# Top-32 attention with two feed-forward layers on one core: the scores of the tile two steps on move from the end of TensorE's step to between its first and second unit

## The chip, the core and the metric

The kernel runs on one core of a Trainium2 chip. The core has five engines that work side by side: TensorE (matmuls), VectorE, ScalarE, GpSimd and SyncE, which here issues nearly all DMAs. Each engine takes its own instructions in the order in which the program lists them, and waits at an instruction until what it needs is there. The metric is the device time of one execution in microseconds (us).

## What is computed

```python
scores = q @ k.T / sqrt(64)                    # 4 batches x 8 heads, 576 x 576
kth    = the 32nd largest of each row of scores
attn   = softmax(where(scores >= kth, scores, -1e9))
x      = attn @ v                              # 2304 tokens x 512
h      = max(x @ w1, x @ w2, x @ w3)           # dense layer, 768 wide
x      = h @ w_out
e      = argmax(x @ w_gate)                    # one of 8 experts per token
out    = gate_weight * (relu(x @ ew1[e]) @ ew2[e])
```

Everything is float32. The kernel keeps precision by splitting a float32 operand into two float16 halves, so that one product takes three matmuls.

## The kernel before, in words

**Tiles and steps.** The score matrix is cut into 144 tiles of 128 rows by 576 columns: 128 "full" ones, and 16 "pair" ones that hold two rests of 64 rows. One loop over `t` (line 1601 and on) is a software pipeline: step `t` does each stage of the attention for another tile. Stages that matter here: the scores of tile `t + 2` (`st_scores`, TensorE, L892), the evacuation of the scores of tile `t + 1` from PSUM to SBUF (`st_evac`, ScalarE, L899), the search for the largest values (`st_chunks` and others, VectorE, L921), threshold passes (ScalarE L967 and L1042, GpSimd L973 and L1045), the exponential and its split in halves (L1051, L1062, L1066), the transpose by DMA (`st_ptr`, SyncE's queue, L1071), and the product with v of tile `t - 14` (`st_av`, TensorE, L1085). Tiles form groups of four; the AV products of a group share one PSUM tile (one buffer), which VectorE reads once the group is done (L1134). The score tile `S` in PSUM has one buffer too, so the scores of tile `t + 2` must wait for the evacuation of tile `t + 1`.

**Units.** When the attention of 128 tokens is done, their dense layer becomes a job of ten units for TensorE: six of `unit_h` (a third of half the dense layer each, 36 matmuls on L355 through the helper `turned`), two of `unit_x2` (the second dense matrix, 9 matmuls on L1178 to L1180), `unit_gate` (12 short matmuls, L1200 to L1202) and `unit_rank` (2 short ones, L1244 and L1245, for the place of each token in its expert's list). Later there are also units of an expert's layers: `unit_e1` (24 matmuls on L355) and `unit_e2` (6 on L366 to L368). A unit writes one of four PSUM tiles `mm`. What reads it is put on the list of the next step or of a later one (`after(1, post)`): a ScalarE copy (L1160 for every third `unit_h`, L1185, L1435), a VectorE maximum (L1163) or a chain of small VectorE operations. In ScalarE's order of a step these copies stand ahead of that step's evacuation, `st_evac`.

**How many units a step does.** `run_units` adds a rate to a credit (1.08 a step at first, later 1.4 and 1.8) and runs units while the credit is positive; a unit of the dense layer costs 1.0, one of an expert 0.67, a gate 0.25 and a rank 0.05. So most steps do one or two big units, and the gate or the rank comes as a small unit ahead of a big one.

**TensorE's order in a step.** Normally: AV, units, four warm-up matmuls on L1710 if credit is left over, scores. In a step where a new group of AV products begins (`fresh`, every fourth), the units come first, then AV, warm-up and scores. These lines of the loop make that order:

```python
if fresh:
    open_slots()
    load_ahead()
    run_units(t)
if ok(n):
    st_av(n)
...
if ok(t + 2):
    st_scores(t + 2)
```

`open_slots` and `load_ahead` issue DMAs on SyncE's queue; `run_units` and `st_scores` issue none. When the attention is over (about 655 us) the loop goes on with units alone, and after it `finale` works off the lists of the experts (from about 787 us).

Of the kernel before, what the change touches and what calls it, by code (L numbers as in the profile page):

```python
# [19 lines left out]
def kernel(  # L20
# [23 lines left out]
    KE = FE // P  # L44
# [13 lines left out]
    UNIT_RATE, TAIL_RATE = 1.08, 2.0  # L58
    NEARLY, NPICK, NMIX, NS1 = 10, 2, 7, 8
    CAP, XA, NSL, NLD, NAHEAD = 1.2, 3, 10, 4, 4  # L60
    NSWAP, XLAG, KLAG, TSTOP, EARLY_RATE, LATE_RATE = 4, 2, 2, 140, 1.4, 1.8
# [33 lines left out]
    def attempt(ctx, general):  # L95
# [18 lines left out]
        def part(n, p=P):  # L114
            o = parts[0]
            parts[0] += n
            return vec[0:p, o:o + n]
# [7 lines left out]
        first = part(NE, 1)  # L125
# [86 lines left out]
        def look_ahead(snap, m8):  # L212

            return [
                lambda: nc.vector.scalar_tensor_tensor(out=m8, in0=snap, scalar=0.0, in1=vrev[0:1, :],
                                                       op0=ALU.is_gt, op1=ALU.mult),
                lambda: nc.vector.scalar_tensor_tensor(out=m8, in0=first, scalar=0.0, in1=m8, op0=ALU.is_equal,
                                                       op1=ALU.mult),
                lambda: nc.vector.max(out=m8, in_=m8),
                lambda: nc.vector.tensor_scalar(out=ahead, in0=m8[:, 0:1], scalar1=-1.0, scalar2=float(NE),  # L220
                                                op0=ALU.mult, op1=ALU.add),
                lambda: nc.vector.tensor_scalar(out=ahead, in0=ahead, scalar1=float(NE - 1), scalar2=None, op0=ALU.min),
                lambda: nc.vector.tensor_copy(out=aheadi, in_=ahead),
            ]
# [402 lines left out]
        with ExitStack() as p1:  # L627
# [40 lines left out]
            def freed():  # L668
                live[0] -= 1
# [9 lines left out]
            def chain(fns):  # L679
                chains.append(list(fns))  # L680
                return chains[-1]
# [66 lines left out]
            def run_late():  # L748
                while late:
                    late.pop(0)()  # L750
# [132 lines left out]
            def st_scores(n):  # L883
                kind, b, qb, h = tiles[n]
                ps = ps_s.tile([P, 2, 512], F32, tag="S", name="S")
                Sps[n] = ps
                qt, (km, kr) = qT[b, qb], kT[b]
                hs = [(h, 0, P)] if kind == "full" else [(h[0], 0, REM), (h[1], REM, REM)]
                for j in range(2):
                    for vv in range(2):  # L890
                        for hh, o, m in hs:
                            nc.tensor.matmul(out=ps[o:o + m, j, 0:(REM if j else NQ * P)], lhsT=qt[:, vv, hh, 0:m],  # L892
                                             rhs=kr[:, hh] if j else km[:, hh // HG, :, hh % HG],
                                             start=(vv == 0), stop=(vv == 1))
# [392 lines left out]
            slots, task, W1h, W1e, eld, hld = [], [], [], [], [], []  # L1287
            ew, e1, e2, half = [], [], [], [None]
# [55 lines left out]
            def load_ahead():  # L1344

                if not looked:
                    if raw and len(ranked) >= NTT - NAHEAD:
                        looked.append(clock[0])
                        chain(look_ahead(ranked[-1].snap, sm_p.tile([1, NE], F32, tag="m8s", name="m8s")))
                elif looked[0] + 1 < clock[0] and n_raw[0] < 2 * KD and len(eld) == KE + 2 * KD:  # L1350
                    w, i = divmod(n_raw[0], KD)
                    n_raw[0] += 1
                    re = nc.sync.value_load(aheadi[0:1, 0:1], min_val=0, max_val=NE - 1)
                    n = (1, KE // KD)[w]
                    nc.sync.dma_start(
                        out=raw[w][:, i * n:(i + 1) * n, :],
                        in_=(ew1, ew2)[w][bass.ds(re, 1), i * n * P:(i + 1) * n * P, :].rearrange(
                            "o (k p) f -> p (o k) f", p=P))
# [132 lines left out]
            credit = [0.0]  # L1491

            def run_unit():
                if run_early():
                    return True
                for j in jobs:
                    if j.ready > clock[0] or (live[0] >= room() and j.u != NU1 + 1):
                        continue
                    if j.u < NU1:
                        unit_h(j, j.u)  # L1500
                        j.ready = clock[0] + (3 if j.u == NU1 - 1 else 0)
                        credit[0] -= 1.0
                    elif j.u < NU1 + 2:
                        unit_x2(j, j.u - NU1)
                        j.ready = clock[0] + (0 if j.u == NU1 else 4)
                        credit[0] -= 1.0
                    elif j.u == NU1 + 2:
                        unit_gate(j)
                        j.ready = 1 << 30
                        credit[0] -= 0.25  # L1510
                    else:
                        unit_rank(j)
                        credit[0] -= 0.05
                    j.u += 1
                    if j.u == NU1 + 4:
                        jobs.remove(j)
                    return True
                return run_late_slot()

            def run_units(t):  # L1520
                credit[0] = min(credit[0] + (TAIL_RATE if e2 else LATE_RATE if len(eld) >= KE else EARLY_RATE if slots
                                             else UNIT_RATE), 2.5 if e2 else CAP)
                while credit[0] > 0 and run_unit():
                    pass


            preps = []
# [20 lines left out]
            def ok(n):  # L1548
                return 0 <= n < NTL
# [8 lines left out]
            with tc.manual_schedule():  # L1558
# [35 lines left out]
                t = -1  # L1594
# [6 lines left out]
                while second is None or not fin() or len(ranked) < NTT:  # L1601
# [89 lines left out]
                    n = t - L_AV  # L1691

                    fresh = ok(n) and n % G == 0
                    if fresh:
                        open_slots()
                        load_ahead()
                        run_units(t)
                    if ok(n):
                        st_av(n)
                        if n % G == G - 1:  # L1700
                            after(1, lambda g=n // G: st_x(g))
                    if not fresh:
                        open_slots()
                        load_ahead()
                        run_units(t)

                    if WARM and 30 <= t < NTL and credit[0] > 0 and live[0] < room() - 1:
                        ps = mm_tile()
                        for _ in range(WARM):
                            nc.tensor.matmul(out=ps, lhsT=ones16, rhs=WO[:, 0, 0, :], start=True, stop=True)  # L1710
                        freed()
                    if ok(t + 2):
                        st_scores(t + 2)
                    run_late()
                    if not picked and len(ranked) >= NPICK:
                        picked = t
# [22 lines left out]
    with ExitStack() as first_time:  # L1739
        attempt(first_time, False)  # L1740
    with tc.If(missed[0] > 0, preferred_fallthrough_block=False):
        with ExitStack() as second_time:
            attempt(second_time, True)
# [29 lines left out]
```

## Time and profile before

| | us |
|---|---|
| median of 3 runs (923.32 to 924.06) | 924.04 |
| the profiled execution | 919.08 |
| its span, first to last instruction | 917.4 |

| engine | busy us | share of the span |
|---|---|---|
| VectorE (DVE) | 745.3 | 81% |
| TensorE matmuls (PE) | 741.1 | 81% |
| ScalarE (ACT) | 705.7 | 77% |
| GpSimd (POOL) | 597.5 | 65% |

The shares are means over stages with different limits. The first 145 us load and split the weights and start the pipeline, and TensorE does little; from 145 to 652 us attention and units run together; the rest is units and experts. In the views, PE is TensorE, DVE VectorE, ACT ScalarE, POOL GpSimd and SPq the DMA queue of SyncE. A line of a timeline gives start, duration, engine, source line, operation, what is written and read, and the count; in square brackets stands how long the engine had been idle before and what ended that.

### The profile page before, as it was taken

The numbers are of one execution on the slowest core, as the hardware profiler recorded it, in microseconds if no ns is written. First come the engines' busy times: TensorE is split into PE (matmuls) and PEld (weight loads), VectorE is DVE, ScalarE is ACT, GpSimd is POOL, SyncE is SP. The second block draws the span as 40 slices with busy tenths as digits, with TensorE's granted clock in tenths as the row PEclk, the third lists the DMA queues.
The fourth block names the chain that finished last, engine by engine and source line by source line (L and its number), as shares of the span: only waits on it lengthen the run. The fifth ranks groups of instructions, "written<-read, shape, count | busy, mean of one in ns | idle before, by whom it ended". The sixth has DMA issues, their size and how long they took to land.

```text
span 917.4 us, 29131 instructions
## 1 busy us (share of the span) xinstructions
PE 741.1 (81%) x10606; PEld 573.4 (63%) x10606; DVE 745.3 (81%) x3108; ACT 705.7 (77%) x1464; POOL 597.5 (65%) x554
## 2 busy tenths in 40 slices
PE   1112367888878799978988899989999999999993
PEld 0000236576655678757767688757987756687882
DVE  5999998999999999999998999998852426476661
ACT  4768999999999999999997999998862231566661
POOL 2556788898988699887877889888992220211110
PEclk9999999999998999999989999999999999999997
DMA  9872977767997888799989788988977459699270
GB/s 223 262 232 51 222 148 152 128 135 133 194 167 162 157 153 169 150 201 173 175 167 172 167 158 155 179 173 148 188 153 128 128 170 298 173 298 258 60 223 16
DMA packets 372164, 155.93 MB, mean 170 GB/s; under 512 B 331931, under 2 KB 348319, under 8 KB 372000
## 3 DMA queue, kind: packets, MB, share of 16 engines
q1 hardware_dynamic: 368128, 143.10, 75.0%
q0 software_dynamic: 3136, 9.46, 3.3%
q8 instruction: 87, 1.43, 0.7%
q10 hardware_dynamic: 736, 1.32, 0.4%
q14 instruction: 77, 0.63, 0.2%
HBM read 76.06 MB, written 16.67 MB: 101 GB/s over the span
## 4 chain that ended last, share of the span: by engine, by line
PE 29%; ACT 20%; issue 19%; DVE 17%; POOL 8%; DMA 4%; SPq 1%; POOLq 0%; ACTq 0%; DVEq 0%
PE mm L355 15%; ACT g L967 4%; DVE c L921 4%; PE av L1085 4%; ACT s L899 3%; PE S L892 3%; ACT e L1051 3%; ACT phl L1062 2%; POOL phl L1066 2%; DVE vec L982 2%; POOL f L973 2%; PE mm L1178 2%; DVE e L1056 2%; PE mm L1179 2%; PE mm L1180 2%
## 5 line engine op out<-in xcount | busy, mean ns | idle before, releaser
L355 PEld LDWEIGHTS <-W 128*128 128x128 f16 x4560 | 248.5, 100 | 19.6 <-issue 16.5
L355 PE MATMUL mm<-xT,W 128*128 128x128 f16 x3456 | 214.3, 224 | 13.3 <-DVE vl L746 5.6
L973 POOL TENSOR_TENSOR f<-s,g 128x576 f32<-128x576 f32 x144 | 184.1, 1278 | 40.4 <-ACT g L967 24.2
L1066 POOL TENSOR_TENSOR phl<-e,phl 128x576 f16<-128x576 f32 x144 | 188.2, 1307 | 6.5 <-ACT phl L1062 5.7
L921 DVE MAX8 c<-s 128x8 f32<-128x96 f32 x864 | 175.0, 243 | 9.4 <-ACT s L899 5.6
L892 PEld LDWEIGHTS <-qT 128*128 128x128 f16 (+1 forms) x640 | 56.6, 107 | 189.8 <-issue 155.2
L892 PE MATMUL S<-kt,qT 128*128 128x64 f16 (+3 forms) x320 | 61.9, 345 | 107.2 <-ACT s L899 91.5
L1051 ACT ACTIVATE e<-s,be 128x576 f32<-128x576 f32 x144 | 109.8, 762 | 14.6 <-POOL phl L1066 10.9
L1085 PE MATMUL av<-vh,pt 128*128 128x65 f16 (+3 forms) x1600 | 110.6, 200 | 11.4 <-DVE xn L1134 9.8
L967 ACT ACTIVATE g<-s,bf 128x576 uint16<-128x576 f32 x144 | 111.7, 775 | 5.6
L982 DVE MAX8 vec<-f 128x8 f32<-128x576 f32 x144 | 108.7, 755 | 4.7 <-POOL f L973 1.9
L1045 POOL TENSOR_TENSOR s<-s,g 128x576 f32<-128x576 f32 x72 | 92.6, 1286 | 24.0 <-DVE e L1056 22.3
L1085 PEld LDWEIGHTS <-pt 128*128 128x128 f16 (+3 forms) x2400 | 89.3, 103 | 24.2 <-issue 11.0
L899 ACT ACTIVATE s<-S 128x576 f32<-128x576 f32 x144 | 91.6, 636 | 12.3 <-PE S L892 11.9
L1062 ACT ACTIVATE phl<-e 128x576 f16<-128x576 f32 x144 | 96.2, 668 | 5.9 <-DMA pt<-phl 5.9
L1085 PE MATMUL av<-vl,pt 128*128 128x64 f16 (+3 forms) x800 | 100.1, 197 | 0.0
L461 DVE SCALAR_TENSOR_TENSOR W<-st,W 128x1024 f16<-128x1024 f32 x56 | 65.8, 1220 | 37.3 <-ACT W L460 28.7
L1056 DVE SCALAR_TENSOR_TENSOR e<-s,hkth,e 128x576 f32<-128x576 f32 x72 | 85.4, 1186 | 12.7 <-ACT e L1051 8.0
L892 PE MATMUL S<-kT,qT 128*128 128x512 f16 (+3 forms) x320 | 48.6, 292 | 22.5 <-ACT s L899 22.4
L1169 POOL TENSOR_TENSOR hhl<-a,hhl 128x384 f16<-128x384 f32 x36 | 37.6, 1046 | 33.5 <-ACT hhl L1168 32.3
L460 ACT ACTIVATE W<-st 128x1024 f16<-128x1024 f32 x56 | 55.6, 1046 | 1.8 <-DMA st<-in_moe_w_dram 1.8
L1042 ACT ACTIVATE g<-s,hkth 128x576 uint16<-128x576 f32 x72 | 54.7, 760 | 0.0
(233 smaller groups left out, 1568.6 us busy)
## 6 DMA issues: line engine op xcount, KB each, us to landing
st<-in_moe_w_dram SPq DMA_DIRECT2D x72, 512.0 KB
st<-in_moe_w_dram SPq DMA_DIRECT2D x28, 256.0 KB
raw<-in_moe_w_dram SPq DMA_DIRECT2D x12, 512.0 KB
st<-in_v_dram SPq DMA_DIRECT2D x16, 256.0 KB
hs<-he SPq DMA_DIRECT2D x16, 256.0 KB
hTe<-hs SPq DMA_DIRECT2D x8, 512.0 KB
st<-in_q_dram SPq DMA_DIRECT2D x15, 256.0 KB
qT<-qT SPq DMA_DIRECT2D x30, 128.0 KB
```

The lines of the kernel that those rows point to most:

```text
L355: nc.tensor.matmul(out=ps[:, o * n:(o + 1) * n], lhsT=w(b, kk, c), rhs=x(a, kk), start=(kk == 0 and i == 0), stop=(kk == KD - 1 and i == 2))
L892: nc.tensor.matmul(out=ps[o:o + m, j, 0:(REM if j else NQ * P)], lhsT=qt[:, vv, hh, 0:m], rhs=kr[:, hh] if j else km[:, hh // HG, :, hh % HG],
L899: nc.scalar.activation(out=s, in_=Sps.pop(n).rearrange("p a b -> p (a b)")[:, 0:S], func=ACTF.Copy, scale=DOWN)
L921: nc.vector.max(out=c[:, i * 8:(i + 1) * 8], in_=s[:, i * CW:(i + 1) * CW])
L967: nc.scalar.activation(out=gg[n], in_=Ss[n], func=ACTF.Sign, bias=bf[g][:, i], accum_out=cnt[g][:, i])
L973: let_in(nc.gpsimd.tensor_tensor(out=ff[n], in0=Ss[n], in1=gg.pop(n).bitcast(F16), op=ALU.subtract))
L982: bulk.append(lambda: nc.vector.max(out=y8[g][:, i, 1:9], in_=y))
L1051: nc.scalar.activation(out=e, in_=Ss.pop(n) if early(n) else Ss[n], func=ACTF.Exp, scale=ESC, bias=be[g][:, i])
L1056: masked.append(nc.vector.scalar_tensor_tensor(out=e, in0=Ss.pop(n), scalar=kth[g][:, i:i + 1], in1=e, op0=ALU.is_ge, op1=ALU.mult))
L1062: nc.scalar.activation(out=ph[:, 0, 0:S], in_=p, func=ACTF.Copy)
L1066: nc.gpsimd.tensor_tensor(out=ph[:, 1, 0:S], in0=p, in1=ph[:, 0, 0:S], op=ALU.subtract)
L1085: nc.tensor.matmul(out=av[o:o + m, i, 0:n], lhsT=t[0:kk, p * NCH + c, o:o + m], rhs=v_rows(x, b, c, hh)[:, 0:n], start=(c == 0 and p == 0 ...
```

## The change

Scores are emitted between the first unit that a step runs and the others. `run_units` gets an argument: its first call in a step adds the rate to the credit and runs at most one unit, then come the scores, and the second call runs the rest. In a fresh step this whole block stands ahead of the AV product, so the scores come ahead of it too. The warm-up matmuls come behind the scores.

```diff
-            def run_units(t):
-                credit[0] = min(credit[0] + (TAIL_RATE if e2 else LATE_RATE if len(eld) >= KE else EARLY_RATE if slots
+            def run_units(t, first):
+                if first:
+                    credit[0] = min(credit[0] + (TAIL_RATE if e2 else LATE_RATE if len(eld) >= KE else EARLY_RATE if slots
                                              else UNIT_RATE), 2.5 if e2 else CAP)
                 while credit[0] > 0 and run_unit():
-                    pass
+                    if first:
+                        break
...
                     fresh = ok(n) and n % G == 0
-                    if fresh:
+                    def units():
                         open_slots()
                         load_ahead()
-                        run_units(t)
+                        run_units(t, True)
+                        if ok(t + 2):
+                            st_scores(t + 2)
+                        run_units(t, False)
+                    if fresh:
+                        units()
                     if ok(n):
                         st_av(n)
                         if n % G == G - 1:
                             after(1, lambda g=n // G: st_x(g))
                     if not fresh:
-                        open_slots()
-                        load_ahead()
-                        run_units(t)
+                        units()
...
-                    if ok(t + 2):
-                        st_scores(t + 2)
                     run_late()
```

## Rows read from the trace of the kernel before

**Rows 1.** Three stretches: busy us of PE, PEld, DVE, ACT, POOL; clock; DMA.
```profile
145.00:608.00 463.00, 407.56 (x6264) 329.58 (x6263) 438.87 (x2101) 433.51 (x958) 397.13 (x345) 0.97 0.86 163
608.00:655.00 47.00, 46.53 (x623) 34.82 (x623) 42.43 (x210) 41.45 (x92) 41.76 (x35) 0.96 0.95 164
655.00:787.00 132.00, 130.37 (x1585) 94.19 (x1585) 60.09 (x227) 52.54 (x101) 51.78 (x59) 1.00 0.72 173
```
**Rows 2.** Waits, 145 to 608 us (SPq to 655): us, times, longest.
```profile
PE S L892 <- ACT s L899: 31.2, 26, 3.1
ACT s L899 <- PE S L892: 6.7, 9, 1.8
ACT xr L1185 <- PE mm L1180: 2.0, 1, 2.0
DVE c L921 <- ACT s L899: 2.5, 6, 0.9
SPq L1071 <- PE av L1085: 29.7, 19, 4.3
```
**Rows 3.** Timeline of step 118 (fresh), and of one single-unit step.
```profile
545.80 0.63 ACT L899 ACTIVATE s<-S 128x576 f32<-128x576 f32 x1
544.77 4.18 PE L355 MATMUL mm<-xT,W 128*128 128x128 f16 x72
549.60 0.66 PE L892 MATMUL S<-kT,qT 128*128 128x512 f16 x4
550.30 0.65 ACT L899 ACTIVATE s<-S 128x576 f32<-128x576 f32 x1 [1.33 <-PE S L892]
569.55 0.65 ACT L899 ACTIVATE s<-S 128x576 f32<-128x576 f32 x1 [0.44 <-PE S L892]
```
**Rows 4.** Timeline of step 133: second unit, scores, ScalarE's next two.
```profile
615.19 2.17 PE L355 MATMUL mm<-xR,W 128*128 128x128 f16 x36
617.20 0.65 PE L892 MATMUL S<-kT,qT 128*128 128x512 f16 x4
617.69 1.23 PE L355 MATMUL mm<-xR,W 128*128 128x128 f16 x19
617.40 0.49 ACT L1160 ACTIVATE a<-mm 128x384 f32<-128x384 f32 x1 [0.53 <-PE mm L355]
617.89 0.65 ACT L899 ACTIVATE s<-S 128x576 f32<-128x576 f32 x1
```
**Rows 5.** Timeline of step 65: rank, two big units, evacuations, VectorE.
```profile
307.43 0.17 PE L1245 MATMUL mm<-oh,ones 128*128 128x8 f16 x1
311.15 5.81 PE L355 MATMUL mm<-xT,W 128*128 128x128 f16 x72 [3.56 <-DVE vl L746]
312.14 0.63 ACT L899 ACTIVATE s<-S 128x576 f32<-128x576 f32 x1
317.49 0.65 ACT L899 ACTIVATE s<-S 128x576 f32<-128x576 f32 x1 [1.82 <-PE S L892]
317.24 1.20 DVE L1163 TENSOR_TENSOR a<-a,mm 128x384 f32<-128x384 f32 x2
```
**Rows 6.** Timeline of step 137: gate's end, scores, SP, ScalarE.
```profile
630.14 0.17 PE L1202 MATMUL mm<-wg,x2T 128*128 128x8 f16 x1
632.75 0.65 PE L892 MATMUL S<-kT,qT 128*128 128x512 f16 x4
625.19 1.42 SPq L1071 DMA_TRANSPOSE pt<-phl  x1
629.15 0.68 ACT L1062 ACTIVATE phl<-e 128x576 f16<-128x576 f32 x1 [1.26 <-DMA pt<-phl]
631.30 0.64 ACT L899 ACTIVATE s<-S 128x576 f32<-128x576 f32 x1
```
**Rows 7.** Granted clock (figure before the last two), and 72 matmuls.
```profile
311.50:314.00 2.50, 2.50 (x28) 2.50 (x26) 1.48 (x10) 2.50 (x10) 1.07 (x2) 0.51 0.83 188
395.60:399.00 3.40, 3.40 (x62) 3.40 (x62) 3.40 (x18) 3.37 (x9) 2.70 (x3) 1.00 1.07 172
395.57 4.18 PE L355 MATMUL mm<-xT,W 128*128 128x128 f16 x72 [1.66 <-DVE he L1436]
```

## The prediction

> **What bounds the kernel now.** I read the table of stretches first [rows 1]. From 145 to 608 us no engine sets the pace alone: of 463 us VectorE is busy 438.87, ScalarE 433.51 and TensorE 407.56. From 608 to 655 TensorE is busy 46.53 of 47 us, and from 655 to 787, where only units and the last AVs are left, 130.37 of 132. So the kernel has two regimes around this change. Up to 608 us the two softmax engines pace it and TensorE has about 55 us of idle time; from 608 us on TensorE has none, and whatever idle time it is given there goes straight to the end. Before 145 us there are no units and TensorE mostly waits; only the AV of every fourth step changes places with the scores there, and I cost that at nothing.
>
> The table of waits comes next [rows 2]. Up to 608 us TensorE waits 31.2 us in front of the scores for ScalarE's evacuation, since the score tile has one buffer. In the other direction ScalarE waits only 6.7 us, in 9 places, for the scores to be done. The change is about these 9 places. VectorE, which takes the evacuated scores, waits 2.5 us for ScalarE there.
>
> Last I read the timeline of single steps. A step lasts about 4.4 us (106 steps, 26 to 131, in 463 us). Its order on TensorE is AV, units, warm-up matmuls, scores; in every fourth step, where a new group of AV tiles begins ("fresh"), it is units, AV, warm-up, scores.
>
> **What the change does to the order.** No instruction is added or removed. Which unit runs in which step is decided by a credit, and the split call adds it once and takes the same units, so only TensorE's order changes; no DMA is issued in the moved code, and what is issued for later steps (the readers of a unit) hangs on the step, not on the place. From the loops, of steps 14 to 141, 44 plain steps have two or more units and 11 have warm-up matmuls behind at most one: there the scores pass the second unit or the warm-up. All 32 fresh steps change: the scores pass the AV too. The other 41 stay as they are.
>
> **The gain, up to 608 us.** Step 118 is the pattern [rows 3]. ScalarE has emptied the score buffer at 545.80 + 0.63 = 546.43. TensorE does both units (4.18 us from 544.77), the AV, and the scores from 549.60; ScalarE has waited 1.33 us when it can start at 550.30. In the new order the scores start behind the first unit, about 546.9, and ScalarE's wait is gone. The ceiling is the 6.7 us, less 0.44 for a step with a single unit (the row at 569.55) [rows 3], 6.3 us. The floor is what VectorE waits for the same evacuations, 2.5 us [rows 2]: where VectorE has work in hand, an earlier ScalarE gives nothing. I take the middle, 4.4 us.
>
> **The loss, up to 608 us.** ScalarE takes its work in order, and the reader of a step's second unit stands in front of the evacuation of the scores in the next step. That unit now ends later, by the scores it lets pass: 617.69 - 617.20 = 0.49 us from their start to the next matmul [rows 4]. Rows 4 is the pattern: the second unit ends at 617.36 and ScalarE, which had waited 0.53 us for it, copies it at 617.40 and evacuates at 617.89. In the new order that copy starts 0.5 us later and the evacuation behind it too, though its scores are long there: the wait has moved from the scores to the unit. Between 145 and 608 us I find nine steps (33, 59, 71, 95, 96, 100, 101, 104, 105) with such a reader close behind its second unit; with 0.2 us of slack on the mean they cost 9 x 0.3 = 2.7 us. Step 59 among them is ScalarE's wait of 2.0 us [rows 2].
>
> Step 65 is a loss of another kind [rows 5]. Its first unit is the ranking, two short matmuls, over at 307.6. The new order then waits for the evacuation (312.14 + 0.63), where TensorE used to start the two big units at 311.15. They would start at 312.77 + 0.5 = 313.3 and end about 5.81 us later, at 319.1. VectorE reads them at 317.24, two readings of 0.6 us, the second at 317.9: it would wait 1.2 us. ScalarE's 1.82 us there is gained, and counted above. The loss is 2.7 + 1.2 = 3.9 us, and between 0 (if the engines are out of step by more than 0.5 us) and 3.9.
>
> AVs of fresh steps come 0.5 us later as well, and SP's transposes wait for AVs (29.7 us in 19 places [rows 2]), with loads queued behind. I cost it at nothing: what is transposed is read two steps, about 9 us, later. If that cover were gone it would be 19 x 0.5 = 9.5 us on SP, which is not the end of any chain I read. The AV's own wait for VectorE (fresh steps) no longer holds up the scores; that is within the gain counted.
>
> So the first stretch gives -4.4 + 3.9 = -0.5 us.
>
> **The cost, 608 to 655 us.** What ScalarE waits for scores there is worth nothing, since TensorE is the bound. What counts is whether TensorE gets new idle time. In most steps the first unit ends after the evacuation. Step 137 is the exception [rows 6]: its first unit is the gate, which ends at 630.14 + 0.17 = 630.31, and the evacuation runs from 631.30 to 631.94. TensorE used to do two expert units in this time, and scores at 632.75 without a wait. Now it waits at the scores, with the two units behind them in its queue: 631.94 - 630.31 = 1.6 us, 1.7 with the start after a wait (0.04 us between 617.36 and 617.40 [rows 4], an estimate for TensorE). That ScalarE may come earlier to it does not help much: it is held up just before, 1.26 us, by a transpose that SP issued at 625.19. Bounds: 0 (evacuation earlier by the whole 1.7) and 1.7; I take 1.7, since the row of the transpose is in the way.
>
> **The sum.** -0.5 + 1.7 = +1.2 us. The rows are of one execution of 919.08 us (span 917.4 and 1.7 around it), 5.0 us below the median of 924.04; I carry the difference over to the median: 925.2 us, which is within the 0.2% (1.85 us) that a measurement of this kernel can tell from no change.
>
> [...]
>
> **The rivals.**
> - ScalarE paces the first stretch: all of 6.3 us comes back and the late readers cost nothing, because the whole step moves ahead of them. For it: ScalarE's waits are real idle time. Against it: VectorE is the busier engine. 924.0 - 6.3 + 1.7 = 919.4 us, faster. Chance 0.24.
> - The second units become the wait: VectorE's 2.5 us is all that is gained, and the 3.9 and 1.7 us are paid: 924.0 - 2.5 + 3.9 + 1.7 = 927.1 us, slower; with no gain at all 929.6. It decides from the point at which more steps have a reader within 0.5 us of its unit than have a wait for the scores. For it: nine against nine. Chance 0.28.
> - The clock falls in the gap of step 137: TensorE, the bound there, loses 5.81 - 4.18 = 1.6 us more, 926.8 us, slower. Against it: the 1.66 us row. Chance 0.08.
> - The change does next to nothing: TensorE waits 31.2 us at the scores in any order, and the place of a wait is all that moves: 924.0 us. Chance 0.10.
>
> **How the numbers follow.** The forecast of 925.2 has 0.30; with the rival that nothing happens, "within 0.2%" has 0.40. Faster has 0.24, slower 0.28 + 0.08 = 0.36. The range goes from the first rival, 919.4, to the far end of the second, 929.6; beyond these the gains or losses would have to exceed every wait that I found.
>
> **What would show it.** In the profile after: ScalarE's waits for the scores nearly gone (right: under 1.5 us in all up to 655); in their place waits of ScalarE for the matmuls of units, 2 to 5 us; TensorE's waits at the scores longer than 31.2 us, with a new one of over a microsecond in step 137, before two expert units; TensorE still without idle time from there to 787. It would be wrong if VectorE's busy share between 145 and 608 rose above 96% (a real gain), if TensorE showed no new gap behind the gate of step 137, or if SP's transposes came so late that ScalarE waited for them more often than now.

## The result and the profile after

The changed kernel takes 935.39 us (median of 6 runs, 931.38 to 939.88) where the kernel before takes 924.05 us beside it: 1.0115 times as long, 95% interval 1.0084 to 1.0147. The change makes the kernel 11 us slower, and the time lies above the whole predicted range. The profiled execution of after took 932.32 us, with a span of 930.6 us; before it was 919.08 and 917.4, so the two traces differ by 13.2 us.

The stretches of the profile of after, in the columns of [rows 1] (stretch, its length, busy us of PE, PEld, DVE, ACT and POOL, granted clock, share of the DMA engines, GB/s). The last row, of a stretch that is looked at below, is followed by the row of before for the same stretch.

```profile
145.00:608.00 463.00, 400.20 (x6104) 323.14 (x6103) 429.11 (x2061) 424.89 (x938) 388.86 (x337) 0.96 0.83 159
608.00:655.00 47.00, 44.37 (x601) 34.20 (x600) 39.23 (x204) 40.35 (x92) 39.58 (x36) 0.96 0.76 155
655.00:787.00 132.00, 130.30 (x1719) 99.17 (x1717) 62.90 (x251) 54.94 (x112) 59.17 (x64) 1.00 0.74 170
...
392.00:470.00 78.00, 64.13 (x907) 52.77 (x905) 67.10 (x307) 65.87 (x145) 58.60 (x52) 0.91 0.87 171
```
```profile
392.00:470.00 78.00, 65.45 (x955) 54.07 (x954) 74.28 (x347) 74.61 (x166) 64.22 (x58) 0.93 0.98 182
```

Against [rows 1], VectorE and ScalarE have done 9.8 and 8.6 us less work between 145 and 608 us. Most of that is missing in one place, 392 to 470 us, where they do 7.2 and 8.7 us less. Before, both of them and the DMA engines were busy 95 to 98% of that stretch. From 608 to 655 us TensorE has 2.2 us more idle time than before, from 655 to 787 no more.

The waits of after, 145 to 608 us (the last row, SyncE's queue, to 655), answer to [rows 2]: us in total, times, longest.

```profile
PE S L892 <- ACT s L899: 60.1, 45, 4.3
DVE c L921 <- ACT s L899: 6.9, 10, 1.8
ACT a L1160 <- PE mm L355: 5.9, 6, 1.7
ACT xr L1185 <- PE mm L1180: 5.8, 4, 2.3
ACT hl L762 <- DMA kT<-hl: 3.2, 1, 3.2
ACT s L899 <- PE S L892: 3.0, 4, 1.2
ACT he L1435 <- PE mm L355: 2.8, 2, 1.6
...
SPq L1071 <- PE av L1085: 53.5, 24, 6.1
```

ScalarE's waits for scores fell from 6.7 to 3.0 us, which is what the change does. In their place ScalarE waits 14.5 us for units (lines 1160, 1185 and 1435; before 2.2, of which 0.2 on line 1160), TensorE 60.1 us in front of the scores (31.2), SyncE's transposes 53.5 us for AVs (29.7).

Where the time goes can be followed with one measure: the start of ScalarE's evacuation (line 899) of the scores of tile n, after less before. Step t evacuates tile t + 1. From n = 24 to 80 this lag goes up and down and comes back to under 1 us: 0.1 us at 34, 1.9 at 44, 0.1 at 50, -0.7 at 68, 0.8 at 80. Then it is 1.2 us at tile 87, 7.2 at 90, 8.4 at 96, 10.3 at 98 and still 10.3 at 101. It falls to 6.8 at 120, and is 8.6 at 138, 10.3 at 140, 11.6 at 142 and 10.0 at 143, the last. So 9 us come from the steps 86 to 96, and up to 3 from the steps 137 to 141. Near 755 us TensorE is 11.1 us behind; the rest is lost later, where it waits 1.9 us longer in all for two DMAs of the experts' inputs. How far the lag moves by itself can be read from the run with step 137 alone (below): up to that step its order is that of before, and its lag lies between -0.8 us (tile 61) and 2.9 us (tile 127). A smaller change of the lag in a single trace shows nothing by itself.

Step 86 is fresh and begins with a job's ranking. This is TensorE there, and then SyncE's queue (start, duration, engine, line, operation; in brackets the idle time before and what ended it):

```profile
396.83 0.17 PE L1245 MATMUL mm<-oh,ones 128*128 128x8 f16 x1
399.63 1.01 PE L892 MATMUL S<-kt,qT 128*128 128x512 f16 x4 [2.63 <-ACT s L899]
400.45 5.48 PE L355 MATMUL mm<-xT,W 128*128 128x128 f16 x72
```
```profile
405.77 0.19 PE L1085 MATMUL av<-vh,pt 128*128 128x65 f16 x1
```
```profile
398.86 1.62 SPq L1071 DMA_TRANSPOSE pt<-phl  x1
400.53 0.57 SPq L729 DMA_DIRECT2D st<-in_k_dram  x1
401.33 2.08 SPq L784 DMA_TRANSPOSE kT<-hl  x1
406.56 1.32 SPq L1071 DMA_TRANSPOSE pt<-phl  x1
409.39 0.38 SPq L1333 DMA_DIRECT2D st<-in_moe_w_dram  x1
409.87 1.39 SPq L721 DMA_DIRECT2D st<-in_k_dram  x1
411.36 1.48 SPq L784 DMA_TRANSPOSE kT<-hl  x1
```

The kernel before had the same AV, P transpose, loads and K transpose here:

```profile
399.59 0.19 PE L1085 MATMUL av<-vh,pt 128*128 128x65 f16 x1
```
```profile
401.44 1.33 SPq L1071 DMA_TRANSPOSE pt<-phl  x1
404.28 0.38 SPq L1333 DMA_DIRECT2D st<-in_moe_w_dram  x1
404.76 0.94 SPq L721 DMA_DIRECT2D st<-in_k_dram  x1
405.80 1.30 SPq L784 DMA_TRANSPOSE kT<-hl  x1
```

The ranking is over at 397.0. The scores wait 2.63 us for the evacuation, and the two large units stand behind them. Behind these stands the AV: 405.77 us, where before it began at 399.59. SyncE's transpose of the next P tile (line 1071) needs the buffer that this AV reads. It is issued at 406.56 (before 401.44), and the expert-weight load, the K load and the K transpose behind it follow 5 us late as well (before 404.28, 404.76, 405.80). Two engines meet the K transpose:

```profile
416.52 0.63 ACT L762 ACTIVATE hl<-st 64x512 f16<-64x512 f32 x1 [3.18 <-DMA kT<-hl]
```
```profile
417.67 0.68 DVE L746 TENSOR_TENSOR hl<-mm,hl 64x512 f16<-64x512 f32 x1 [2.83 <-ACT mm L745]
```

ScalarE's line 762 splits the next piece of K into a buffer that the late transpose still reads; before, it waited 0.27 us there.

### The profile page after: what moved, and what is told of

It is laid out like the page before. It is cut to its first block, busy times and chain, and to the rows that moved or that the text cites. A ratio compares the mean times of both kernels' runs of the same rounds, so it can differ in the third digit from the quotient of the medians.

```text
span 930.6 us, 29090 instructions
## 1 busy us (share of the span) xinstructions
PE 741.7 (80%) x10606; PEld 575.7 (62%) x10606; DVE 743.0 (80%) x3108; ACT 705.0 (76%) x1464; POOL 596.5 (64%) x554
## 4 chain that ended last, share of the span: by engine, by line
PE 28%; DVE 22%; issue 19%; ACT 18%; POOL 6%; DMA 5%; SPq 1%; POOLq 0%; DVEq 0%; ACTq 0%
PE mm L355 14%; DVE c L921 5%; ACT s L899 3%; PE av L1085 3%; DVE vec L982 3%; PE S L892 3%; DVE e L1056 3%; ACT g L967 3%; ACT e L1051 2%; ACT phl L1062 2%; PE mm L1178 2%; ACT mm L745 2%; PE mm L1180 2%; PE mm L1179 2%; POOL f L973 1%
## 5 line engine op out<-in xcount | busy, mean ns | idle before, releaser
L1085 PE MATMUL av<-vh,pt 128*128 128x65 f16 (+3 forms) x1600 | 108.5, 200 | 0.5 <-DMA pt<-phl 0.3
L1056 DVE SCALAR_TENSOR_TENSOR e<-s,hkth,e 128x576 f32<-128x576 f32 x72 | 82.9, 1151 | 12.3 <-ACT e L1051 11.5
```

The source lines that it names most:

```text
L1056: masked.append(nc.vector.scalar_tensor_tensor(out=e, in0=Ss.pop(n), scalar=kth[g][:, i:i + 1], in1=e, op0=ALU.is_ge, op1=ALU.mult))
L1085: nc.tensor.matmul(out=av[o:o + m, i, 0:n], lhsT=t[0:kk, p * NCH + c, o:o + m], rhs=v_rows(x, b, c, hh)[:, 0:n], start=(c == 0 and p == 0 ...
```

## Experiments

Two theories for the 11 us. **A, the late AV:** in a fresh step the AV comes behind the scores' wait and the held-up units; SyncE's queue stands still until it is done, and the loads behind come late. **B, the late units:** large units stand behind the scores' wait, and their readers on ScalarE and VectorE come late, over many steps. Most kernels below choose for each step the old or the new order, by this edit of the changed kernel and one condition:

```diff
+                    split = CONDITION
                     def units():
...
-                        if ok(t + 2):
+                        if split and ok(t + 2):
                             st_scores(t + 2)
...
                         freed()
+                    if not split and ok(t + 2):
+                        st_scores(t + 2)
                     run_late()
```

Each time is a median, with the kernel before timed beside it on the same chip (it took 918.5 to 921.6 us in these groups); the ratio has its 95% interval. It is taken from all the runs of the two kernels, so it need not be the quotient of the two medians. The expectations give times for a kernel before of 924 us; where it took 921.3 beside the first four runs, they are read here as differences from it.

**The old order in fresh steps.**

```diff
+                    split = not fresh
```

> The changed kernel, but the 32 fresh steps keep the old order (all units, AV, scores). Theory A (late AV): in a fresh step the AV now stands behind the scores and the held-up units, SP's next P transpose waits for that AV, and the loads and K transposes queued behind it come late to ScalarE; this is some 9 of the 11.3 us. Expected by A: 925 to 928 us, what is left being the gap of step 137. Theory B (late second units): the loss comes from units held up behind the scores' wait, in plain and fresh steps alike, whose readers on ScalarE and VectorE come late: 931 us or more.

928.84 us, ratio 1.0086 (1.0065 to 1.0107), 7.5 us above before, where A had 1 to 4 and B 7 or more: B's figure, and a miss for A as the only cause. In its trace the lag still grows from 3.4 us (tile 87) to 7.5 (tile 98), three quarters of it from tile 92 on, in plain steps.

**The old order in step 86.**

```diff
+                    split = t != 86
```

> The changed kernel, with the old order in step 86 alone. Step 86 is fresh and begins with the ranking, so that the scores' wait, two units and the AV stood behind each other there. Theory A (late AV), if this one step begins the loss: 926 to 929 us, and the trace shows no wait of ScalarE's split for the K transpose near 417 us. Theory B (late second units, spread over many steps): 934 to 935.5 us.

926.83 us, ratio 1.0062 (1.0040 to 1.0083), 5.5 us above before; A had 2 to 5 and B 10 or more. ScalarE's wait for the K transpose there falls from 3.2 to 1.0 us, and between tiles 87 and 101 the lag grows by 3.6 us instead of 9.0. So roughly half of that is step 86, and the rest is something else.

**The new order in step 86 alone.**

```diff
+                    split = t == 86
```

> The kernel before, with the new order in step 86 alone. Theory A (late AV): most of the loss is made here, 929 to 933 us. Theory B (late second units over many steps): 924 to 926 us.

925.36 us, ratio 1.0050 (1.0028 to 1.0072). One step costs some 4 us, between B's 0 to 2 and A's 5 to 9. Its trace shows the chain again, TensorE first and then ScalarE (the first of ScalarE's three waits, at 402.87, is for a K transpose issued at 400.74, ahead of the held one, and is not part of the chain):

```profile
399.04 1.12 PE L892 MATMUL S<-kt,qT 128*128 128x512 f16 x4 [4.48 <-ACT s L899]
399.96 5.64 PE L355 MATMUL mm<-xT,W 128*128 128x128 f16 x72
```
```profile
402.87 0.63 ACT L762 ACTIVATE hl<-st 128x512 f16<-128x512 f32 x1 [1.66 <-DMA kT<-hl]
409.47 0.65 ACT L899 ACTIVATE s<-S 128x576 f32<-128x576 f32 x1 [1.45 <-PE S L892]
415.34 0.63 ACT L762 ACTIVATE hl<-st 64x512 f16<-64x512 f32 x1 [2.32 <-DMA kT<-hl]
```

**Gate and ranking don't count as first unit.** The scores come behind the first large unit, which covers the evacuation.

```diff
...
-                    if first:
+                    if first and big[0]:
                         break
```

(`big` is set when the unit took more than half a credit.)

> The changed kernel, but gate and ranking don't count as a step's first unit: the scores come behind the first large unit. In steps 86, 92 and 137 a large unit then covers the evacuation. Theory A (late AV): the AV of step 86 is late by the scores alone, 0.5 us, so the loss there goes, and so does the gap of step 137: 923 to 926 us. If already an AV that is 0.5 us late blocks SP, as fresh steps have it everywhere: 930 us or more. Theory B (late second units): only the 18 steps with a gate or a ranking first are changed, a gain of 3 to 5 us: 930 to 932 us.

921.74 us, ratio 1.0005 (0.9986 to 1.0025), which is A's figure (-1 to 2 us above before) and not B's (6 to 8): the loss is not spread over all steps, but lies in steps whose first unit is a gate or a ranking. Within those steps it tells nothing between a late AV and late units, since both are on time again.

**Step 86, the AV ahead of the scores.** Only the AV moves against the run with step 86 alone: ranking, AV, scores, two units.

```diff
+                    split = t == 86
...
+                        if split:
+                            st_av(n)
                         if split and ok(t + 2):
                             st_scores(t + 2)
...
                     if ok(n):
-                        st_av(n)
+                        if not split:
+                            st_av(n)
```

> The kernel before, with step 86 alone in the order ranking, AV, scores, the two large units. Against the run with step 86 alone in the new order (4.0 us slower than before) only the AV moves, ahead of the scores' wait; the two units stay held up behind it. Theory A (the late AV blocks SP): SP's transpose of step 87 is issued at 401 to 402 us instead of 406.2, the late K transpose goes, and of the 4 us no more than 2 are left. Theory B (the late units): SP is early as in A, but the time stays 3.5 to 5 us above before.

920.21 us, ratio 1.0008 (0.9992 to 1.0023). The units stay late, and ScalarE waits for one of them and for late scores (waits of ScalarE, 396 to 425 us: total, times, longest):

```profile
ACT a L1160 <- PE mm L355: 2.5, 1, 2.5
ACT s L899 <- PE S L892: 0.9, 1, 0.9
```

The lag rises from 0.5 us at tile 87 to 4.1 at tile 89 and is back to 2.0 at tile 92: of what the late units lose here, the next steps make good about half in the trace, and by time 0.7 us are left, which can't be told from nothing. The transpose of line 1071 is issued at 401.93, and no wait for the K transpose is left. Step 86 is A's.

**Steps 92 and 96 alone.**

```diff
+                    split = t in (92, 96)
```

> The kernel before, with the new order in steps 92 and 96 alone: plain steps, the first with the gate, the second with the ranking as first unit. In the changed kernel with the old order in step 86 the evacuations fell 3.6 us back between steps 87 and 103. If that is these two steps: 3 to 4 us above before, with ScalarE waiting for the large unit of step 92 and for the expert unit of step 95 or 96. If it is the sum of many small delays in plain steps with two large units: 0 to 1 us above before.

922.69 us, ratio 1.0031 (1.0011 to 1.0050), in accord with the first expectation. Step 92, with the gate first, in its trace (the first fence TensorE and its granted clock over the held-up unit, the second ScalarE):

```profile
429.59 1.12 PE L892 MATMUL S<-kt,qT 128*128 128x512 f16 x4 [1.41 <-ACT s L899]
...
430.60:433.40 2.80, 2.80 (x37) 2.80 (x35) 2.70 (x16) 2.25 (x4) 2.79 (x3) 0.65 0.55 125
```
```profile
433.71 0.49 ACT L1160 ACTIVATE a<-mm 128x384 f32<-128x384 f32 x1 [0.86 <-PE mm L355]
438.89 0.65 ACT L899 ACTIVATE s<-S 128x576 f32<-128x576 f32 x1 [1.25 <-PE S L892]
```

The unit runs at a granted clock of 0.65 and takes 3.15 us instead of 2.17 (before, at 1.00), its reader waits 0.86 us, and two steps on the scores themselves are late, 1.25 us. The lag grows by 2.3 us at tiles 94 and 95 and keeps that to tile 101; step 96 adds 0.2. ScalarE's two waits are for a late unit and for scores that stand behind units, as B has it. SyncE's transpose waits for a late AV here too (3.6 us in one place between 424 and 452 us, where the kernel before has no such wait), but no compute engine waits for a DMA in that stretch. So the trace speaks for B in these steps; no run parts the two.

**Step 137 alone.**

```diff
+                    split = t == 137
```

> The kernel before, with the new order in step 137 alone. The prediction's own term: TensorE waits about 1.7 us behind the gate and has no idle time after, so 1.7 us above before. Rival: ScalarE is not ahead of its evacuation by this order, but what it does next comes earlier and the gap shrinks: 0 to 0.5 us. If TensorE's clock falls in the gap: 2.5 to 3.5 us.

921.56 us, ratio 1.0008 (0.9990 to 1.0027; the two medians lie 2.3 us apart): a loss of 1.7 us and none are both within the interval. The gap is there, and the granted clock behind it was 1.00 in one execution and 0.61 in another. First the changed kernel, then this one: the scores behind the gate, and the granted clock while the two expert units behind them run.

```profile
640.60 0.65 PE L892 MATMUL S<-kT,qT 128*128 128x512 f16 x4 [1.68 <-ACT s L899]
...
641.10:643.80 2.70, 2.70 (x16) 1.26 (x15) 2.60 (x18) 2.70 (x6) 2.27 (x3) 1.00 0.72 91
```
```profile
634.12 0.65 PE L892 MATMUL S<-kT,qT 128*128 128x512 f16 x4 [1.45 <-ACT s L899]
...
634.60:639.00 4.40, 4.40 (x16) 1.71 (x15) 4.30 (x22) 4.37 (x10) 3.94 (x5) 0.61 0.95 133
```

With the clock at 1.00 the two units take 1.46 us each, with 0.61 over both of them 2.51 and 2.14: the profiled execution here pays 3.5 us, where after pays the 1.7 of the gap. In five profiled executions with the new order in this step (after, the old order in fresh steps, the old order in step 86, step 137 alone, and the AV behind the first unit, below) the gap was 1.68, 1.69, 1.68, 1.45 and 1.69 us; of two of them the clock behind it is shown, 1.00 in after (1.68 us) and 0.61 here (1.45 us).

**The new order only where the first unit is large.** The steps with a gate or a ranking first keep the old order. In the trace of before there are 24 of them in steps 37 to 140, 13 with a gate and 11 with a ranking; the expectations count 18.

```diff
...
+                        split[0] = run_units(t, True) is not False
+                        if split[0] and ok(t + 2):
                             st_scores(t + 2)
...
+                    if not split[0] and ok(t + 2):
+                        st_scores(t + 2)
```

(`run_units` returns False when the first unit was a gate or a ranking.)

> The changed kernel, but steps whose first unit is a gate or a ranking keep the old order altogether; the scores come behind the first unit only where that is a large one. If all of the loss is in the 18 small-first steps, what is left is the gain of the change: ScalarE's waits for scores, 2.5 to 6 us: 915 to 919 us where before gives 921.3. If the held-up second large units cost as much as those waits give, as the prediction had it: 920 to 922.5 us.

920.30 us, ratio 1.0016 (0.9998 to 1.0035): no gain that can be told from nothing, as the second expectation has it. Between 145 and 655 us ScalarE's waits for scores fall from 9.8 to 4.6 us in it, and its waits for units at line 1185 rise from 2.0 to 7.8.

**All fresh steps, the AV behind the first unit.** First unit, AV, scores, other units.

```diff
                         run_units(t, True)
+                        if fresh:
+                            st_av(n)
                         if ok(t + 2):
...
                     if ok(n):
-                        st_av(n)
+                        if not fresh:
+                            st_av(n)
```

> The changed kernel, but in fresh steps the AV comes right behind the first unit, ahead of the scores: first unit, AV, scores, the other units. Theory A (the late AV of fresh steps blocks SP, above all in step 86): the part of step 86 goes, as it did when this step alone was changed so, and about 5 to 8 of the 11.3 us are left (steps 92, 96 and 137 and the plain steps). Theory B (held-up units alone): 10 us or more are left.

935.35 us, ratio 1.0165 (1.0134 to 1.0197): a miss for A, which had 5 to 8 us left, and no proof for B either. Step 86 behaves as A says (the lag at tile 90 is 3.7 us, not 7.2). But the first AV of a group waits for VectorE to read the group before it, and the second unit now stands behind that wait, as well as the scores: 5.9 us in 4 places up to 655 us (before 5.4 in 4 up to 608, behind the units), and then twice where TensorE is the bound.

```profile
682.79 0.19 PE L1085 MATMUL av<-vh,pt 128*128 128x65 f16 x1 [2.98 <-DVE xn L1134]
```
```profile
717.51 0.19 PE L1085 MATMUL av<-vh,pt 128*128 128x65 f16 x1 [2.28 <-DVE vec L1272]
```

The granted clock was 0.96 from 655 to 700 us (1.00 in before and in after). How the 17 us divide was not followed further.

**Steps 112 to 118 alone,** where the lag falls by 3.4 us in the trace of after.

```diff
+                    split = 112 <= t <= 118
```

> The kernel before, with the new order in steps 112 to 118 alone, where ScalarE waited for scores (the evacuations of 116, 118 and 120) and where, in every trace with the new order there, the evacuations gained 3.4 to 3.6 us on the kernel before between steps 112 and 120. If an earlier ScalarE lasts to the end: 2 to 3.5 us under before, faster than both kernels. If it is given back before TensorE becomes the bound: within 1 us of before.

919.59 us, ratio 1.0003 (0.9986 to 1.0021). In its trace the evacuations gain 2.2 us between tiles 114 and 120, 1.5 of which are given back at tiles 121 and 122. A gain of up to 1.3 us is not excluded, but none is measured, and no kernel here is faster than the one before.

**All but steps 86, 92, 96 and 137.**

```diff
+                    split = t not in (86, 92, 96, 137)
```

> The changed kernel, with the old order in steps 86, 92, 96 and 137 alone. If the loss is in these four steps, as the single runs say (4.0 us for step 86, 2.9 for 92 and 96, about 1 to 3 for 137), 0 to 2 us above before are left. If the other small-first steps or the large second units cost as much again: 3 us or more above before.

922.99 us, ratio 1.0019 (0.9995 to 1.0042). Four of the 87 steps that change their order carry most of the loss; the 2 us that are left (interval -0.5 to 3.9) can't be told from nothing. The length of TensorE's wait at the scores doesn't tell which steps these are: in the trace of after it is 2.63 us in step 86, 2.40 in 92 and 1.68 in 137, but 4.20 in step 65, 3.02 in step 130 and 2.27 in step 100, which keep the new order here.

**Step 86 alone, SyncE's blocked transpose one step later.** The AV stays late, the loads pass.

```diff
                     n = t - L_PTR
+                    if t == 88:
+                        st_ptr(n - 1)
-                    if ok(n):
+                    if ok(n) and t != 87:
                         st_ptr(n)
...
+                    split = t == 86
```

> The kernel before with the new order in step 86 alone (4.0 us slower than before), and SP's P transpose of step 87, the one that waits for the late AV, issued one step later, behind the expert-weight load, the K load, the K transpose and the two attention-output transposes that stood behind it. The AV stays late, and so do the units. If the late AV costs through SP's queue: these loads are issued at about 405 us instead of 409, ScalarE's wait for the K transpose near 415 us goes, and 0 to 2 us above before are left. If it costs in another way, or if the units are what costs: 3 to 5 us above before.

924.53 us, ratio 1.0037 (1.0020 to 1.0054): a miss for A. The trace does show what A said of the queue: the expert weights are loaded at 403.51 us, K at 404.35, and ScalarE's wait for the K transpose is gone. But two P transposes now follow each other (3.36 us from 409.11), ScalarE waits 0.70 us for one of them, and the lag at tile 97 is 2.7 us above that of tile 87, against 4.3 with step 86 alone and 1.8 with the AV ahead. By time most of the loss of step 86 stays, although the loads are early. The edit delays a second P transpose, a cost of its own, so it doesn't decide.

**Step 86 with the AV ahead, but its last matmul behind the units.** TensorE does the same work in the same order, but for one of the AV's 15 matmuls, and the P tile is free only after the units.

```diff
...
                         if split:
-                            st_av(n)
+                            st_av(n, 0)     # all but the last matmul
                         if split and ok(t + 2):
                             st_scores(t + 2)
                         run_units(t, False)
+                        if split:
+                            st_av(n, 1)     # the last matmul
```

> The run with step 86 in the order ranking, AV, scores, units (0.8 us above before), with one thing changed: the last of the AV's 15 matmuls is issued behind the two units. TensorE's work and the place of the scores and units stay, but the P tile that the AV reads is free only after the units, and SP's transpose of step 87 waits for that. If the late AV costs through what waits for its tile (SP's transpose and the loads behind it): the transpose is issued at about 406 us again, ScalarE waits for the K transpose near 415 us, and the time is 3 to 5 us above before. If it costs through TensorE's own order: 0 to 1.5 us above before, as without this edit.

924.80 us, ratio 1.0042 (1.0026 to 1.0058), against 1.0008 without this edit and 1.0050 with step 86 alone: the loss is back, by one matmul. SyncE waits for it, and everything behind is late (SyncE's wait, three of its DMAs, ScalarE's wait, 396 to 425 us):

```profile
SPq L1071 <- PE av L1088: 3.9, 1, 3.9
```
```profile
405.58 1.32 SPq L1071 DMA_TRANSPOSE pt<-phl  x1
408.41 0.38 SPq L1336 DMA_DIRECT2D st<-in_moe_w_dram  x1
408.90 0.70 SPq L721 DMA_DIRECT2D st<-in_k_dram  x1
```
```profile
ACT hl L762 <- DMA kT<-hl: 2.8, 1, 2.8
```

(The edit moves some line numbers by three.) So in step 86 the late AV costs through the tile that it holds and what waits for that in SyncE's queue, not through TensorE's order. Which of the queue's members makes the loss, the late P transpose itself or the loads and the K transpose behind it, is not shown: the run before this one had the loads early and the P transpose late, and 3.4 us (interval 1.8 to 5.0) remained. The lag of the evacuations over these steps, in four traces:

| tile | step 86 alone | AV ahead | AV ahead, last matmul behind | transpose later |
|---|---|---|---|---|
| 87 | 0.6 | 0.5 | 0.3 | 0.5 |
| 89 | 3.9 | 4.1 | 3.3 | 4.4 |
| 90 | 6.0 | 3.7 | 5.8 | 4.9 |
| 92 | 4.9 | 2.0 | 4.3 | 3.1 |
| 97 | 5.0 | 2.3 | 4.3 | 3.1 |

Up to tile 89 all four lose 3 to 4 us, with the late units that they share. By tile 92 the run whose P tile is free early has got half of it back. The two whose tile is held have not, and the run with the transpose out of the way lies between. These are single executions, with the spread told above.

## Why the prediction was wrong

**The step that failed** is the one that cost the late AVs at nothing. It had two premises. The first was that AVs of fresh steps come 0.5 us later, by the scores alone. In step 86 the AV came 6.2 us later, 5 without the 1.2 us that the traces were apart already: the scores' wait (2.63 us) and the scores (0.8) now stood ahead of the two units and the AV, and the units took 5.48 us instead of the 4.18 of [rows 7], which shows this very step before the change; the granted clock was 0.60 from 400.45 to 403.90 us. The second premise was that the cover is the two steps until the transposed P tile is read. What counted was the queue: the transpose waited for the tile that the late AV held, and an expert-weight load, a K load and a K transpose came as late behind it, in a stretch where both softmax engines were 95% busy. That the held tile makes the loss is shown by one matmul (1.0008 and 1.0042); how it divides between the P transpose and the loads is open. The price of that cover being gone, which the prediction gave as 9.5 us on a queue that "is not the end of any chain I read", is by chance close to what after loses in steps 86 to 96: about half of that is this chain (some 4 us by time), most of the other half the next point.

**The small-first steps.** The prediction saw that a ranking as first unit leaves large units behind the wait, priced step 65 at 1.2 us and step 137 at 1.7, and took no other for that (step 96 is among its nine steps with a close reader, at 0.3 us). There are 24 steps with a gate or a ranking first. Two of them, 92 and 96, cost 2.9 us together (ratio 1.0031, interval 1.0 to 4.6 us): in the trace readers of late units, a granted clock of 0.65, and late scores after that. Step 65 itself shows no cost that can be told from the spread of the lag: it falls by 1.9 us at tile 67 (and by 1.6 in a trace that leaves step 65 as it was).

**The gain.** The change did take ScalarE's waits for scores away, though not to under 1.5 us (3.0 are left, up to 608), and the gain of 4.4 us was not there: where only large first units are affected the kernel is no faster (1.0016, 0.9998 to 1.0035), and the stretch of steps 112 to 118, which gained in its trace, gave most of it back. The forecast's own balance of this part, nearly nothing, held; the 2 to 5 us of waits for units became 14.5.

**Step 137.** The gap came as foretold, 1.68 us for 1.7, and TensorE had no idle time after it. The rival that the clock falls there, with the difference of the 72 matmuls of [rows 5] and [rows 7] as its cost, was too small at 0.08: it came true in one of the two executions whose clock is shown (0.61 and 1.00), at a cost of 1.7 us; the single gap of 1.66 us in [rows 7] was no ground for so small a chance. And the rival looked at step 137 alone: the units of step 86 took 1.3 us longer too, at that clock of 0.60, and that of step 92 1.0 us (3.15 for 2.17), at 0.65. By time, the step's cost is not settled between none and 2.5 us.

**The sum,** by ratios: step 86 0.50%, steps 92 and 96 0.31%, step 137 0.08%, all the rest 0.19% make 1.08%, and the change measured 1.15%. The parts add up within their intervals, each of about 0.2% to either side. One sign against the forecast that its last paragraph names came true, transposes so late that ScalarE waits for them: up to 655 us it waits 4.0 us in 4 places for P transposes (before 2.9 in 3) and 3.2 us for the K transpose (before 0.3).

Of the rivals, the second, with the units as the wait, had the right sign and a part of the mechanism (steps 92 and 96). Its far end was 929.6 us, since it knew of no way in which a late unit or AV could hold up a queue.

## What to carry to other kernels

When work is moved ahead of something that waits, price everything that then stands behind that wait, in the steps where the piece meant to cover it is small: here 4 of 87 steps carried most of the loss. For each instruction that becomes late, follow the buffer it releases, not only the result it makes: here a DMA that waited for the buffer held up what was queued behind it (the expert-weight load began at 409.39 us instead of 404.28), and that may be nearer to the bound than the DMA's own reader. In step 86 a delay of the units alone cost next to nothing by time (ratio 1.0008), and with the buffer held for as long as the units it cost 0.4%; but late units are not always harmless: in steps 92 and 96 they went with a loss of 0.3%.

## What the runs showed of the hardware

Nearly the same gap of TensorE, at the same place, was followed by a granted clock of 1.00 in after (1.68 us) and of 0.61 in the run with step 137 alone (1.45 us), over the two units behind it. So the length of the gap alone doesn't decide: the shorter of the two was followed by the lower clock. (In step 92 a gap of 1.41 us was followed by 0.65, but there the clock had been at 0.50 before the gap already, behind a wait of 2.76 us.) What else decides is not shown.

SyncE's queue was stopped by its first waiting member: in five traces with an early or a late AV (before, after, step 86 alone, AV ahead, last matmul behind) the expert-weight load began 1.50 to 1.51 us after the end of the P transpose ahead of it, wherever that was, from 404.28 to 409.39 us; with that transpose moved behind it, the load began at 403.51 us.
